# VectorE's queue in a channel mixer: weight decodes placed behind the small steps of the latest w_ch2 scale

## The chip, the cores and the metric

The kernel runs on one core of a Trainium2 chip, in one launch. The metric is the device time of one execution in microseconds. The core's engines each work through a queue of their own in order: TensorE (PE, matmuls; PEld is its weight load), VectorE (DVE), ScalarE (ACT), GpSimd (POOL) and SyncE (SP), which requests the transfers here.

## What is computed

The reference chains a causal attention, a token and channel mixer and a gated mixer (batch 2, 448 tokens, 768 channels, 12 heads). The change touches the channel mixer's second half and the load of the gated mixer's first weight:

```python
u = x + (relu(x.T @ w_tok1) @ w_tok2).T        # x: attention's output, 2 x 448 x 768
y = u + relu(u @ w_ch1) @ w_ch2                # w_ch1 768 x 1536, w_ch2 1536 x 768
h = gelu(y @ w_in)                             # w_in 768 x 1024: halves w_inu and w_inv
u2, v = split(h)                               # v is normalised, mixed over tokens, times u2
out = y + gated @ w_out
```

w_tok1, w_tok2, w_ch1, w_ch2, w_in and w_out arrive as 64-bit floats and are turned into 32-bit ones on the chip; the other inputs are 32-bit.

## The kernel before, in words

A weight is loaded by `decode` (L104): one transfer (L113, on SP) into one of two raw buffers `wraw`, a ScalarE pass (L120) over the high words, and two VectorE instructions, a shift (L123) and a shift with an OR (L124), which joins the low words. L124 is the last reader of the raw buffer, so the transfer after the next waits for it.

For accuracy a product is made of three matmuls (`mm3`, L174 to L181: high by high, high by low, low by high). From the channel mixer's second half on, high and low are fp16 with one scale for a whole slice. `spread` (L156) makes a scale: a small matmul (L158) brings the maxima of all partitions together, then come three small VectorE steps, a maximum (L159), a clamp and product (L160) and a reciprocal (L161). I call them the scale's small steps.

The second half runs over m = 0 to 5, 128 output channels each, and two batches. `channel_down(m, ws, [b])` (L226) is one group of 36 matmuls y_ps (L178 to L180), which reads r (the first half's output, split to fp16) and ws[m], the fp16 halves of slice m of w_ch2. An eviction on VectorE (L233, yt), an addition on GpSimd (L235) and a maximum on VectorE (L146, yam) follow. TensorE's groups come in the order (0,0), (1,0), (0,1), (2,0), (1,1), (3,0), (2,1), (4,0), (3,1), (5,0), (4,1), (5,1), written (m, batch).

A slice of w_ch2 takes two functions. `load_w2(m)` (L546) decodes it in two halves (tiles w2m, four buffers), has ScalarE sum up absolute values (L553), and takes the larger sum (L151, w2am) as the bound. `end_w2(m)` (L557) calls `spread`, which makes scale m, and `split16p` (L168): ScalarE multiplies by the scale (L170) and copies to fp16 (L171), and GpSimd subtracts for the low half (L172).

The loop at L607 interleaves these. In round m it traces: group (m, 0); in round 0 the split of r of batch 1 (`split_r`, twelve splits on ScalarE L165 and VectorE L166); `load_w2(m + 3)`; group (m - 1, 1); `end_w2(m + 2)`; the decode of slice m of w_inv (two in round 4, tile wv, six slices of 512) with its maximum (wvam). After the loop come the scale of w_inv, three slices of w_in's other half (`begin16`, tile wm, maximum wams), the last groups, and `to16(b)`, which spreads the maximum of all y of a batch and splits y. Then the v stage begins (L672).

What sets the order of each engine's queue is a planner: it runs a model of the kernel when the program is built, and of the instructions that are ready in the model it prefers the one traced first. `tc.issue_after(ins)` adds an edge: what the block traces on the engine of `ins` is queued behind `ins`. It makes no engine wait for another, and does nothing to the instructions of other engines.

Of the kernel before, what the change touches and what calls it, by code (L numbers as in the profile page):

```python
# [24 lines left out]
TOP = 32768.0  # L25
# [3 lines left out]
def mixer_kernel(  # L29
# [18 lines left out]
    nc = tc.nc  # L48
# [7 lines left out]
    NCC = C // P  # L56
# [47 lines left out]
    def decode(m, src, twice=False):  # L104


        n = src.shape[-1]
        raw = wpool.tile([P, WC], mybir.dt.int64, tag="wraw", name="wraw", bufs=2)[:, :n]
        if twice:
            nc.sync.dma_start(raw[:64], src)  # L110
            nc.sync.dma_start(raw[64:], src)
        else:
            last_load[0] = nc.sync.dma_start(raw, src).ins  # L113
        words = raw.bitcast(I32).rearrange("p (n w) -> p n w", w=2)
        mi = m.bitcast(I32)

        nc.scalar.activation(  # L120
            m, words.bitcast(F32)[:, :, 1], AF.Prelu, scale=2.0 ** -112, alpha=-(2.0 ** 32)
        )
        nc.vector.tensor_scalar(mi, mi, 3, None, ALU.logical_shift_left)  # L123
        nc.vector.scalar_tensor_tensor(mi, words[:, :, 0], 29, mi, ALU.logical_shift_right, ALU.bitwise_or)  # L124
# [19 lines left out]
    def absmax(dst, src):  # L144

        return nc.vector.tensor_reduce(dst, src, AX.X, ALU.max, apply_absolute_value=True)  # L146

    def top_of(cols, name):

        am = stp16.tile([P, 1], BF16, name=name)  # L150
        last_top[0] = nc.vector.tensor_reduce(am, cols, AX.X, ALU.max).ins  # L151
        return am
# [3 lines left out]
    def spread(pm, am, inv, s, top):  # L156

        nc.tensor.matmul(pm[:, :P], am.to_broadcast([P, P]), ident_b, start=True, stop=True)  # L158
        nc.vector.reduce_max(inv, pm[:, :P], axis=AX.X)  # L159
        nc.vector.tensor_scalar(inv, inv, 1e-20, 1.0 / top, ALU.max, ALU.mult)  # L160
        nc.vector.reciprocal(s, inv)  # L161

    def split16(hi, lo, src, s):

        nc.scalar.activation(hi, src, AF.Copy, scale=s)  # L165
        nc.vector.scalar_tensor_tensor(lo, src, s, hi, ALU.mult, ALU.subtract)  # L166

    def split16p(hi, lo, m, s):  # L168

        nc.scalar.activation(m, m, AF.Copy, scale=s)  # L170
        nc.scalar.copy(hi, m)  # L171
        nc.gpsimd.tensor_sub(lo, m, hi)  # L172
# [40 lines left out]
    def channel_up(m, batches, pool, psum):  # L213

        wh, wl = load_w(w_ch1[m])
        for b in batches:
            us = slice(b * S, (b + 1) * S)
            pr = psum.tile([P, 512], F32, tag="d", name="r_ps")
            mm3(pr[:, :S], [((wh[:, c, :], wl[:, c, :]), (u_hi[c][b], u_lo[c][b])) for c in range(NCC)])
            r = pool.tile([P, S], F32, tag=f"r{m}_{b}", name="r")  # L220
            nc.scalar.activation(r, pr[:, :S], AF.Relu, accum_out=rsum[:, b, m:m + 1])
            r_of[m, b] = r
# [284 lines left out]
    wv32 = wvp.tile([P, NCC, DH], F32, name="wv32")  # L507
# [5 lines left out]
    w2sc = [[sc.tile([P, 1], F32, name=f"w2{n}{m}") for n in ("inv", "s")] for m in range(NCC)]  # L513
    w2sum = sc.tile([P, NCC, 2], F32, name="w2sum")
    yam = sc.tile([P, B, NCC], F32, name="yam")
    wvam = sc.tile([P, NCC], F32, name="wvam")
# [10 lines left out]
    with rs:  # L527
        ps_d = ctx.enter_context(tc.tile_pool(name="ps_d", bufs=8, space=PSUM, reuse_waits="tile"))
        r1pool = rs.enter_context(tc.tile_pool(name="r1pool", bufs=1, reuse_waits="tile"))
        tmp = rs.enter_context(tc.tile_pool(name="tmp", bufs=3, reuse_waits="tile"))  # L530
        def pst(name):
            return ps_d.tile([P, 512], F32, tag="d", name=name)

        def split_r(b):

            am = top_of(rsum[:, b], f"ram{b}")
            spread(pst("rs_ps"), am, *rsc[b], TOP)
            for c in range(NFF):
                if b == 0:
                    t = r1pool.tile([P, 2, S], F16, name=f"r16_{c}")  # L540
                else:
                    t = (rpool if c < NF0 else r1pool).tile([P, 2, S], F16, tag=f"r{c}_0", name=f"r16_{c}")
                split16(t[:, 0], t[:, 1], r_of[c, b], rsc[b][1][:, 0:1])
                r_of[c, b] = t

        def load_w2(m):  # L546

            ms = []
            for i in range(2):
                w = tmp.tile([P, WC], F32, tag="w2m", name="w2m", bufs=4)  # L550
                decode(w, w_ch2[m, :, i * NCC:(i + 1) * NCC, :].rearrange("p a f -> p (a f)"))
                unused = tmp.tile([P, WC], BF16, tag="w2a", name="w2a", bufs=1)
                nc.scalar.activation(unused, w, AF.Abs, accum_out=w2sum[:, m, i:i + 1])  # L553
                ms.append(w)
            w2_begun[m] = ms, top_of(w2sum[:, m], f"w2am{m}")

        def end_w2(m):  # L557

            ms, am = w2_begun.pop(m)
            spread(pst("w2_ps"), am, *w2sc[m], TOP)  # L560
            ws[m] = []
            for i, w in enumerate(ms):
                if m < 2:
                    t = tmp.tile([P, 2, NCC, P], F16, name=f"w2_{m}{i}", bufs=1)
                else:
                    t = wpool.tile([P, 2, NCC, P], F16, tag=("whi", "wlo")[i], name="w2", bufs=3)
                split16p(*(t[:, h].rearrange("p a f -> p (a f)") for h in range(2)), w, w2sc[m][1][:, 0:1])
                ws[m] += [(t[:, 0, c, :], t[:, 1, c, :]) for c in range(NCC)]

        w2_begun, ws, w16, begun = {}, {}, {}, []  # L570
        tail = 4
        for m in [*range(NF0 - tail), *range(NF0, NFF), *range(NF0 - tail, NF0)]:
            channel_up(m, [1] if m < NF0 else [0, 1], r1pool, ps_d)
            if m == NF0 + 1:
                with tc.issue_after(last_load[0]):
                    load_w2(0)
            if m == NFF - 2:
                end_w2(0)
                load_w2(1)
            if m == NF0 - tail:  # L580
                end_w2(1)
                split_r(0)
            if m == NF0 - 1:
                load_w2(2)

        def to16(b):

            spread(pst("ys_ps"), yam16[b], *ysc[b], TOP)
            nc.vector.tensor_mul(vinv[:, 2 * b:2 * b + 1], ysc[b][0], wvsc[0])
            hs = slice(64 * b, 64 * b + 64)  # L590
            nc.vector.tensor_copy(vinv[hs, 1:2], vinv[hs, 2 * b:2 * b + 1])
            for m in range(NCC):
                y16[m][b] = upool.tile([P, 2, S], F16, tag=f"ul{m}_{b}", name=f"y16_{m}_{b}")
                split16(y16[m][b][:, 0], y16[m][b][:, 1], y32[m][b], ysc[b][1][:, 0:1])
                ts = slice((1 - b) * (S - 64), (1 - b) * (S - 64) + 64)
                nc.vector.tensor_copy(y3[:, :, m, 64 * b:64 * b + 64], y16[m][b][:, :, ts])

        def begin16(src, j):

            k = src.shape[1]  # L600
            m = wpool.tile([P, WC], F32, tag="wm", name="wm", bufs=3)[:, :k * P]
            decode(m, src.rearrange("p a f -> p (a f)"))
            am = wams[:, j:j + 1]
            absmax(am, m)
            begun.append((j, k, m, am))

        for m in range(NCC):  # L607
            channel_down(m, ws[m], [0], ps_d, tmp)
            if m == 0:
                with tc.issue_after(mms[0, 0][NFF // 2]):  # L610
                    split_r(1)
            if m + 3 < NCC:
                load_w2(m + 3)
            if 0 < m < NCC - 1:
                channel_down(m - 1, ws[m - 1], [1], ps_d, tmp)
            if m + 2 < NCC:
                end_w2(m + 2)
            for c in ([m], [m], [m], [m], [m, m + 1], [])[m]:
                decode(wv32[:, c, :], w_inv[:, c, :])
                absmax(wvam[:, c:c + 1], wv32[:, c, :])  # L620
            if m == NCC - 2:
                wvam16 = top_of(wvam, "wvam16")
        spread(pst("wv_ps"), wvam16, *wvsc, TOP)
        for c in range(NCC):
            split16(wvh[:, c, :], wvl[:, c, :], wv32[:, c, :], wvsc[1][:, 0:1])
        for m in range(3):
            begin16(w_inu[m], m)
        channel_down(NCC - 2, ws[NCC - 2], [1], ps_d, tmp)
        to16(0)
        channel_down(NCC - 1, ws[NCC - 1], [1], ps_d, tmp)  # L630
        last_y = last_top[0]
# [71 lines left out]
    am = gp.tile([P, 1], BF16, name="sg_am")  # L703
# [125 lines left out]
```

## Time and profile before

| | |
|---|---|
| median of 3 runs | 428.0 us (427.85 to 429.33) |
| the profiled execution | 429.78 us, of which the span is 427.8 us |
| TensorE busy | 396.2 us, 93% of the span |
| VectorE busy | 286.9 us, 67% |
| ScalarE busy | 248.2 us, 58% |
| GpSimd busy | 206.2 us, 48% |
| mean granted TensorE clock | 0.975 of full speed |

The page cuts the span into 40 slices of 10.7 us and gives a busy share for each. Shares over the whole span say little about one stage, so the stage of the second half, 231 to 322 us, is read from the timeline and from tables over stretches. In a timeline a row tells where an instruction began, how long it lasted, its engine, line and tiles, and in brackets how long the engine had been idle ahead of it and what released it.

### The profile page before, as it was taken

Reading aid. Unit: us, or ns where it says so; the run is one execution under the profiler, and the core shown is the slowest. Engines: PE = TensorE matmul, PEld = TensorE weight load, DVE = VectorE, ACT = ScalarE, POOL = GpSimd, SP = SyncE. Lnnn points to the kernel's source line nnn. Section 1 sums busy time; section 2 is a strip of 40 time slices with the busy share of each in tenths; the row PEclk is TensorE's granted clock in tenths of the full one; section 3 lists DMA queues with packets and bytes.
Section 4 is the critical chain, followed back from the end, with each engine's and each line's share of the span. In section 5 each row is a group of like instructions: output and inputs, shape, how many; then the busy total and the mean of one; then the engine's idle time right before and its main releaser. Section 6 shows DMA issues by size and latency. Waiting matters only on the chain.

```text
span 427.8 us, 7292 instructions
## 1 busy us (share of the span) xinstructions
PE 396.2 (93%) x2610; PEld 268.7 (63%) x2610; DVE 286.9 (67%) x689; ACT 248.2 (58%) x481; POOL 206.2 (48%) x211
## 2 busy tenths in 40 slices
PE   5978899797899999999999999996999999999996
PEld 3546687674788999999887545542454445544553
DVE  5969666798945635434357997778696897557832
ACT  3979767587976555654779755434064575661200
POOL 2785848587866573431453145241611566228300
PEclk9989899996999999999999999999799999999999
DMA  7999788999956744665540503455403022100122
GB/s 221 200 299 214 163 155 172 245 262 247 266 120 153 174 145 152 221 223 188 180 149 0 185 13 111 154 169 187 141 0 88 0 100 98 51 1 0 66 106 87
DMA packets 61459, 60.99 MB, mean 143 GB/s; under 512 B 47856, under 2 KB 53104, under 8 KB 61424
## 3 DMA queue, kind: packets, MB, share of 16 engines
q1 hardware_dynamic: 61424, 60.54, 52.5%
q8 instruction: 20, 0.33, 0.3%
q14 instruction: 15, 0.12, 0.1%
HBM read 46.50 MB, written 2.75 MB: 115 GB/s over the span
## 4 chain that ended last, share of the span: by engine, by line
PE 35%; DVE 23%; DMA 15%; issue 9%; POOL 8%; ACT 8%; SPq 1%; POOLq 0%; ACTq 0%; DVEq 0%
DMA wraw<-in 7%; PE r_ps L179 5%; PE r_ps L180 5%; PE r_ps L178 5%; DMA pT<-hl 4%; DMA vr<-in 3%; PE s_ps L330 3%; DVE r L166 3%; DVE pe L335 3%; DVE wm L124 2%; PE o_ps L180 2%; PE o_ps L178 2%; PE o_ps L179 2%; DVE w2m L124 2%; POOL hl L357 2%
## 5 line engine op out<-in xcount | busy, mean ns | idle before, releaser
L330 PE MATMUL s_ps<-k,q 128*128 128x64 f32 (+3 forms) x216 | 59.7, 425 | 8.5 <-DMA q<-in 4.7
L357 POOL TENSOR_TENSOR hl<-pe,hl 128x512 f16<-128x512 f32 x43 | 52.9, 1236 | 27.6 <-ACT hl L356 25.5
L100 POOL TENSOR_TENSOR wlo<-wm,whi 128x768 fp32r<-128x768 f32 x19 | 37.7, 1984 | 42.0 <-ACT whi L133 42.0
L178 PE MATMUL y_ps<-r,w 128*128 128x448 f16 x144 | 51.5, 359 | 4.2 <-ACT w L171 4.2
L178 PE MATMUL r_ps<-uh,whi 128*128 128x448 f32 x144 | 53.6, 372 | 0.0
L179 PE MATMUL r_ps<-ul,whi 128*128 128x448 f32 x144 | 53.3, 370 | 0.0
L180 PE MATMUL r_ps<-uh,wlo 128*128 128x448 f32 x144 | 53.0, 368 | 0.0
L179 PE MATMUL y_ps<-r,w 128*128 128x448 f16 x144 | 51.7, 359 | 1.0 <-DVE r L166 1.0
L180 PE MATMUL y_ps<-r,w 128*128 128x448 f16 x144 | 51.3, 358 | 1.1 <-POOL w L172 1.1
L120 ACT ACTIVATE wm<-wraw 128x768 f32<-128x768 f32 (+2 forms) x35 | 27.9, 797 | 41.0 <-DMA wraw<-in 25.2
L123 DVE TENSOR_SCALAR wm<-wm 128x768 int32<-128x768 int32 (+2 forms) x35 | 20.8, 593 | 44.3 <-ACT wm L120 44.3
L330 PEld LDWEIGHTS s_ps<-k,q 128*128 128x128 f32 x216 | 34.1, 218 | 19.9 <-issue 5.5
L335 DVE CUSTOM_DVE_ANT_0 pe<-s_ps,mask 128x192 f32<-128x192 f32 (+3 forms) x84 | 34.9, 443 | 7.9 <-PE s_ps L330 7.7
L124 DVE SCALAR_TENSOR_TENSOR wm<-wraw,wm 128x768 int32<-128x768 int32 (+2 forms) x35 | 37.4, 1068 | 0.5
L235 POOL TENSOR_TENSOR y<-yt,ul 128x448 f32<-128x448 f32 x12 | 15.1, 1262 | 45.6 <-DVE yt L233 45.6
L344 ACT ACTIVATE pe<-pe,bias 128x448 f32<-128x448 f32 (+3 forms) x74 | 35.3, 526 | 0.3
L381 PE MATMUL x_ps<-vh,pT 128*128 128x65 f16 (+1 forms) x240 | 26.1, 198 | 7.4 <-DMA pT<-hl 6.6
L172 POOL TENSOR_TENSOR w<-w2m,w 128x768 f16<-128x768 f32 x12 | 21.8, 1834 | 22.3 <-ACT w L171 13.2
L356 ACT CAST hl<-pe 128x512 f16<-128x512 f32 x43 | 26.1, 611 | 8.6 <-DMA pT<-hl 7.7
L381 PEld LDWEIGHTS <-pT 128*128 128x128 f16 (+1 forms) x240 | 21.2, 98 | 13.8 <-DMA pT<-hl 8.8
L179 PEld LDWEIGHTS r_ps<-ul,whi 128*128 128x128 f32 x144 | 27.0, 188 | 2.7 <-issue 0.4
L180 PEld LDWEIGHTS r_ps<-uh,wlo 128*128 128x128 f32 x144 | 27.0, 188 | 2.7 <-issue 0.2
(205 smaller groups left out, 1022.7 us busy)
## 6 DMA issues: line engine op xcount, KB each, us to landing
wraw<-in SPq DMA_DIRECT2D x35, 768.0 KB, 4.5
wraw<-in SPq DMA_DIRECT2D x14, 512.0 KB, 3.7
vr<-in SPq DMA_DIRECT2D x12, 320.0 KB, 3.8
k<-in SPq DMA_DIRECT2D x12, 224.0 KB, 3.1
q<-in SPq DMA_DIRECT2D x24, 112.0 KB, 3.2
out<-ob SPq DMA_DIRECT2D x12, 224.0 KB, 1.9
wraw<-in SPq DMA_DIRECT2D x3, 256.0 KB, 3.4
pT<-hl SPq DMA_TRANSPOSE x43, 3.9
```

What stands on the lines that cost most here:

```text
L100: nc.gpsimd.tensor_sub(lo, src, f32(hi))
L120: nc.scalar.activation(m, words.bitcast(F32)[:, :, 1], AF.Prelu, scale=2.0 ** -112, alpha=-(2.0 ** 32))
L124: nc.vector.scalar_tensor_tensor(mi, words[:, :, 0], 29, mi, ALU.logical_shift_right, ALU.bitwise_or)
L178: nc.tensor.matmul(ps, lh, rh, start=i == 0 and not begun, stop=False)
L179: nc.tensor.matmul(ps, lh, rl, start=False, stop=False)
L180: done.append(nc.tensor.matmul(ps, ll, rh, start=False, stop=i == n - 1).ins)
L330: nc.tensor.matmul(ps[:, o:o + m], qp[:, q0:q0 + P], k2[:, ks], start=True, stop=True)
L335: nc.vector.tensor_tensor_reduce(out=pe[:, cs], in0=ps[:, cs], in1=mask0 if i == 0 else mask[:, MASKS[i]], scale=-1.0 / math.sqrt(D), scal ...
L344: nc.scalar.activation(pe[:, cs], pe[:, cs], AF.Exp, bias=bias[:, j:j + 1], scale=-1.0)
L356: nc.scalar.copy(hl[:, 0], pe)
L357: nc.gpsimd.tensor_sub(hl[:, 1], pe, hl[:, 0])
L381: nc.tensor.matmul(o, ph, vh[:, c, h, :D + 1], start=j == 0, stop=False)
```

## The change

`spread` returns its reciprocal, and `end_w2` hands it on. In the loop `load_w2(m + 3)` is traced after group (m - 1, 1) and `end_w2(m + 2)`, no longer before them, and it stands with the w_inv decodes in a block whose VectorE instructions are queued behind the reciprocal of the latest w_ch2 scale. In rounds 4 and 5 that is still scale 5's. The three `begin16` of w_in go behind scale 5's reciprocal too. Nothing is added to or removed from what the engines execute.

```diff
         nc.vector.tensor_scalar(inv, inv, 1e-20, 1.0 / top, ALU.max, ALU.mult)
-        nc.vector.reciprocal(s, inv)
+        return nc.vector.reciprocal(s, inv).ins
...
-            spread(pst("w2_ps"), am, *w2sc[m], TOP)
+            done = spread(pst("w2_ps"), am, *w2sc[m], TOP)
...
+            return done
...
-            if m + 3 < NCC:
-                load_w2(m + 3)
             if 0 < m < NCC - 1:
                 channel_down(m - 1, ws[m - 1], [1], ps_d, tmp)
             if m + 2 < NCC:
-                end_w2(m + 2)
-            for c in ([m], [m], [m], [m], [m, m + 1], [])[m]:
-                decode(wv32[:, c, :], w_inv[:, c, :])
-                absmax(wvam[:, c:c + 1], wv32[:, c, :])
-            if m == NCC - 2:
-                wvam16 = top_of(wvam, "wvam16")
+                spread_last = end_w2(m + 2)
+            with tc.issue_after(spread_last):
+                if m + 3 < NCC:
+                    load_w2(m + 3)
+                for c in ([m], [m], [m], [m], [m, m + 1], [])[m]:
+                    decode(wv32[:, c, :], w_inv[:, c, :])
+                    absmax(wvam[:, c:c + 1], wv32[:, c, :])
+                if m == NCC - 2:
+                    wvam16 = top_of(wvam, "wvam16")
...
-        for m in range(3):
-            begin16(w_inu[m], m)
+        with tc.issue_after(spread_last):
+            for m in range(3):
+                begin16(w_inu[m], m)
```

## Rows read from the trace of the kernel before

**Rows 1.** The page's slices: TensorE's busy tenths and its granted clock.

```profile
PE   5978899797899999999999999996999999999996
PEclk9989899996999999999999999999799999999999
```

**Rows 2.** TensorE's waits, 225 to 345: line, releaser, total us, times, longest.

```profile
PE y_ps L178 <- ACT w L171: 4.2, 1, 4.2
PE y_ps L180 <- POOL w L172: 1.1, 2, 0.9
PE y_ps L179 <- DVE r L166: 1.0, 2, 0.6
```

**Rows 3.** Busy table of tile y_ps, four groups: stretch, us, PE, DVE, PEclk, DMA.

```profile
266.75:273.60 6.85, 6.85 (x37) 0.97 (x2) 1.00 0.70 228
280.50:287.60 7.10, 6.88 (x37) 0.67 (x1) 1.00 0.41 124
...
294.60:308.75 14.15, 9.10 (x37) 1.35 (x2) 0.76 0.51 165
```

**Rows 4.** Timeline of TensorE, 277 to 316.

```profile
280.43 0.22 PE L158 MATMUL w_ps<-ident_b,w2am 128*128 128x128 bf16 x1
...
294.31 0.35 PE L180 MATMUL y_ps<-r,w 128*128 128x448 f16 x1
298.86 0.56 PE L178 MATMUL y_ps<-r,w 128*128 128x448 f16 x1 [4.19 <-ACT w L171]
...
303.98 0.44 PE L180 MATMUL y_ps<-r,w 128*128 128x448 f16 x1
...
315.66 0.22 PE L158 MATMUL ys_ps<-ident_b,yam 128*128 128x128 bf16 x1
```

**Rows 5.** Timeline of VectorE, 280 to 305.

```profile
280.53 0.94 DVE L123 TENSOR_SCALAR wv<-wv 128x512 int32<-128x512 int32 x1 [2.08 <-ACT wv L120]
...
288.10 0.43 DVE L123 TENSOR_SCALAR wv<-wv 128x512 int32<-128x512 int32 x1 [0.87 <-ACT wv L120]
...
292.51 0.68 DVE L233 SCALAR_TENSOR_TENSOR yt<-y_ps,yinv,uh 128x448 f32<-128x448 f32 x1
293.11 0.28 DVE L159 TENSOR_REDUCE w2inv<-w_ps 128x1 f32<-128x128 f32 x1
293.30 1.92 DVE L124 SCALAR_TENSOR_TENSOR wm<-wraw,wm 128x768 int32<-128x768 int32 x1
...
296.13 0.15 DVE L161 RECIPROCAL w2s<-w2inv 128x1 f32<-128x1 f32 x1
...
303.41 0.96 DVE L146 TENSOR_REDUCE wams<-wm 128x1 bf16<-128x768 f32 x1
```

**Rows 6.** Timelines of ScalarE and GpSimd, 293 to 303.

```profile
296.32 1.76 ACT L170 ACTIVATE w2m<-w2m,w2s 128x768 f32<-128x768 f32 x2 [1.84 <-DVE w2s L161]
...
293.27 1.14 POOL L235 TENSOR_TENSOR y<-yt,ul 128x448 f32<-128x448 f32 x1 [7.83 <-DVE yt L233]
298.94 3.62 POOL L172 TENSOR_TENSOR w<-w2m,w 128x768 f16<-128x768 f32 x2 [4.53 <-ACT w L171]
```

**Rows 7.** Timeline of VectorE, 234 to 256.

```profile
234.96 0.78 DVE L123 TENSOR_SCALAR w2m<-w2m 128x768 int32<-128x768 int32 x1 [0.63 <-ACT w2m L120]
...
237.24 0.96 DVE L124 SCALAR_TENSOR_TENSOR w2m<-wraw,w2m 128x768 int32<-128x768 int32 x1
...
240.03 0.15 DVE L161 RECIPROCAL w2s<-w2inv 128x1 f32<-128x1 f32 x1
...
249.43 5.55 DVE L166 SCALAR_TENSOR_TENSOR r<-r,rs,r 128x448 f16<-128x448 f32 x3
```

**Rows 8.** Waits of ScalarE, 225 to 345.

```profile
ACT wv L120 <- DMA wraw<-in: 9.2, 5, 4.0
```

**Rows 9.** TensorE's waits, 340 to 428.

```profile
PE w_ps L158 <- DVE wams L146: 1.0, 1, 1.0
PE gt_ps L158 <- DVE gtam L151: 0.6, 1, 0.6
```

## The prediction

> **What bounds the kernel now.** I read the slices of the page first. TensorE is at nine tenths or more from slice 12 to slice 39, but for slice 28, where it drops to six tenths; its granted clock drops to seven tenths in the slice behind that [rows 1]. So TensorE sets the time of this half, and a change can win only what TensorE loses somewhere. The table of its waits from 225 to 345 us says what it loses there: 4.2 us, once, for ScalarE's fp16 copy of a w_ch2 slice (L171), 1.1 us for GpSimd's rest of one (L172), 1.0 us for the splits of r [rows 2].
>
> Next I cut the stage into its twelve groups of matmuls (a group is one m and one batch, 36 matmuls). An undisturbed group takes 6.85 us; the one from 294.60 to 308.75, which is m = 5 of batch 0, takes 14.15 us at a mean granted clock of 0.76 [rows 3]. **So 14.15 - 6.85 = 7.3 us are lost in this one group.** TensorE's timeline shows how: the last matmul of the group before starts at 294.31, the next at 298.86, after 4.19 us of idle time, and at 298.86 and 303.98 a matmul lasts 0.56 and 0.44 us, against 0.35 at 294.31 [rows 4]. With the 4.2 us and at most 1.1 us of waits [rows 2] 7.3 - 5.3 = 2.0 us or a little more are left: the price of the lower clock behind the idle stretch.
>
> Then I ask why the slice was late. TensorE spread its maximum at 280.43 [rows 4]. VectorE takes that up (L159) only at 293.11, and the reciprocal starts at 296.13 [rows 5]. So 12.7 us pass ahead of the first small step, and 3.0 us within three steps that last 0.15 to 0.28 us. The rows between say why: VectorE's queue holds decodes of w_inv and w_in ahead of L159, and one more between the small steps [rows 5]. These come at the pace of their transfers: ScalarE, which opens each decode, waits 9.2 us in all for raw w_inv data [rows 8], and VectorE stands behind it. After the reciprocal ScalarE scales and copies from 296.32, and GpSimd subtracts twice from 298.94, 3.62 us for both [rows 6]; the first half is whole at 298.94 + 1.81 = 300.75, 4.6 us after the reciprocal began.
>
> **The change part by part.**
>
> *Scale 5 gets ahead of the decodes.* Slices 3, 4 and 5 of w_inv and the three of w_in are queued behind the reciprocal of scale 5. What then stands ahead of its L159 is the eviction of group (2, batch 1), 0.68 us, now at 292.51 [rows 5], which can run as soon as TensorE ends that group near 280.5. The reciprocal then starts at about 280.5 + 0.7 + 0.3 + 0.15 = 281.7, say 282, and the first half is whole at 286.6. TensorE wants it near 294.5. **The two waits and the low clock go, 7.3 us, with 8 us in hand.** ScalarE could eat into that by standing at a raw slice ahead of the scaling; its longest such wait is 4.0 us [rows 8].
>
> *Scale 4 gets ahead of slice 5 and of slice 2 of w_inv.* Group (4, batch 0) lasts 7.10 us with 6.88 busy [rows 3]; these 0.22 us may go. I count nothing.
>
> *Slice 3 of w_ch2 gets behind scale 2.* Now its halves are decoded from 234.96, in some 0.78 + 0.96 us each, and scale 2's reciprocal follows at 240.03 [rows 7]. Afterwards both halves start behind 240, in the window where twelve splits of r for batch 1 are due, and group (0, batch 1) already waits 1.0 us for these [rows 2]. Bounds: below, a gain of 1.0, since ScalarE now stops for the first w_inv slice ahead of the splits; above, both halves get in front of the splits, 2 x 1.74 = 3.5 us. I take 0, the nearer end: the splits are traced earlier than the slice, so that the planner prefers them whenever both are ready, and ScalarE delivers them one right behind another.
>
> *The requests move with the decodes.* Each L113 on SP waits for the L124 that frees one of two raw buffers; their order stays. The edge holds VectorE's part alone: L120 on ScalarE has none. Behind the held decodes wait ScalarE's sum of a slice (L553) and SP, behind which only the loads of b_sg and w_sg are queued. The decodes behind scale 5 could begin at 282 rather than 280.53; at (288.10 - 280.53) / 2 = 3.8 us for a slice [rows 5] the last of w_inv ends near 291 and the last of w_in near 303. TensorE spreads the scale of w_inv behind group (5, batch 0), 301.4 afterwards, and those of w_in in the v stage. No wait follows.
>
> *GpSimd subtracts for scale 5 near 285 to 289*, beside w_inv decodes, not beside the last of w_in. An L124 that starts beside a GpSimd addition takes 1.92 us (293.30 [rows 5], 293.27 [rows 6]), a lone one 0.96 [rows 7]. So a microsecond or two of VectorE's time moves from one place to another, with no TensorE wait behind it.
>
> *Downstream* everything is released by TensorE's own results, and from 340 on it waits only 1.0 and 0.6 us [rows 9]. So the 7.3 us should reach the end.
>
> **Sum.** The profiled run took 429.78 us, 427.80 of it span and 1.98 around it: 427.80 - 7.3 = 420.5 of span, 422.5 with what lies around. The median of the runs shown is 428.00, 1.78 below the profiled run; the same 7.3 taken from it gives **420.7 us**.
>
> **The rivals.**
>
> *The wait moves.* Group (5, batch 0) now ends at 294.5 + 6.9 = 301.4 and (4, batch 1) at 308.25, where TensorE spreads the maximum of batch 0's y (now at 315.66 [rows 4]). That hangs on the eviction of (5, batch 0). If the planner leaves this behind the last w_in slice, whose maximum ends at 303.41 + 0.96 = 304.4 [rows 5], and behind one or two other evictions (0.68 [rows 5], addition 1.14 [rows 6], maximum at most the 0.96 of a w_in slice: 2.8 each), its own 2.8 us end at 310.0 or 312.8, and TensorE waits 1.7 or 4.5 us: 422.4 to 425.2. The other place is the bound above: 3.5 us at the splits of r, 424.2. For it speaks that VectorE's queue runs 12 us behind TensorE's results here (280.5 against 292.51); against it that it is the decodes that hold it up, and that these now come later in the plan, while evictions don't.
>
> *Slower: the w_ch2 slices become one chain.* Slice 3 waits for scale 2, scale 3 for slice 3, and so on to scale 5, whose spread is a matmul in TensorE's queue: if slice 5 is late, TensorE stands there. Eight pieces (two halves each of slices 3, 4 and 5, and two w_inv slices) have to pass between 240.03 [rows 7] and 280.43 [rows 4]. At 4 us each (3.8 by rows 5) plus a pass of ScalarE for the sum, about the 0.88 of one scaling [rows 6], and the maximum, that is 33 of 40 us. If slice 3 only starts behind the splits of r, at 249.4 to 255 [rows 7], the chain ends at 282.6 to 288.2, and TensorE waits 2.2 to 7.8 us, with 2 more for the clock. From 5.3 us of wait on the change loses; at the far end it loses 7.8 + 2 - 7.3 = 2.5 us, and with the two L124 of slice 3 at 1.92 rather than 0.96 a further 1.9: 430.5 to 432.4. For it: the last three splits took 5.55 us [rows 7], so VectorE can be slow there. Against it: not all eight come at the pace of transfers, since a request goes out as soon as a raw buffer is free.
> The Trainium skill (SBUF — State Buffer, section Who interferes with whom) speaks against the change at this place: a VectorE instruction with two SBUF inputs is fully blocked by a GpSimd instruction that reads SBUF, and slice 3's L124 would move from a time in which GpSimd idles to the one in which it subtracts for scale 2. By that rule each L124 would wait out a whole subtraction; the 5.55 us agree with it. The prices above stand without it.
>
> *Given back.* The v stage and the gates behind it become the bound, as VectorE's work there doesn't shrink, and the time stays at 428. Against it: TensorE's short waits from 340 on [rows 9]. The same time comes out if the change doesn't do what it says, which only the planner could bring about: the decodes do stand ahead of scale 5's steps in the queue [rows 5].
>
> **How the numbers follow.** The forecast, 419 to 422: 0.56. The wait moves in part, 422 to 425.8: 0.20. Given back, 425.9 to 430.1: 0.10. Slower, by the chain: 0.14. The measurement can tell about 0.5%, 2.1 us, from no change. So faster is 0.56 + 0.20 = 0.76, same 0.10, slower 0.14. The range begins at 428 - 7.3 - 1.0 - 0.2 = 419.5, less 0.5 for the scatter of the runs, 419.0, and goes to 427.0, which leaves out the slower case and part of the one that gives all back.
>
> **What would show it.** Right: L159 of scale 5 within 2 us of its spread; no wait of TensorE for L171 or L172 over 0.5 us; group (5, batch 0) at 6.9 us with a clock of 1.00; the v stage from about 315. Wrong: a wait of TensorE at a spread of w2am; longer waits for r; evictions of batch 0 behind w_in; new waits once the v stage has begun.

## The result and the profile after

The changed kernel takes 423.45 us (median of 4 runs, 422.21 to 424.69) against 427.93 us before (427.66 to 429.33): a ratio of 0.989, 95% interval 0.985 to 0.993. So it is 4.5 us faster, inside the range on record (419.0 to 427.0), but 2.75 us behind the 420.7 us that were taken as likeliest, and outside the 419 to 422 us that had the highest chance. All ratios here and below leave out single runs that took over 1.5% longer than the fastest run of their kernel, such as 428.01 us in e5 and 433.79 us in e9. Most of the forecast gain came, and part of it was taken away again at another place.

The profiled execution took 422.21 us with a span of 420.1 us. Its span is 7.7 us shorter than that of before, which is more than the medians differ, so I cut both spans at two events: the first y_ps matmul, where the second half of the channel mixer begins, and the first v_ps matmul, where it ends.

| | first y_ps | first v_ps | second half | from there to the end |
|---|---|---|---|---|
| before | 231.2 | 322.5 | 91.3 | 105.3 |
| after | 228.2 | 314.9 | 86.7 | 105.2 |

The part ahead of the first y_ps scatters from execution to execution: it was 228.2 and 229.3 us in two profiles of the changed kernel, 231.2 and 231.7 us in two kernels below that also gain (e1, e2), and 228.4 us in one (e9) whose time is that of before. So the 3.0 us there are within that scatter and are not put down to the change. **The change is worth 91.3 - 86.7 = 4.6 us in the second half**, which agrees with the medians, and this length is what I compare from here on.

The page's slices, TensorE's busy tenths and its granted clock. The 6 in slice 28 and the clock's 7 behind it [rows 1] are gone; a 7 stands in slice 24 now, and a clock of 8 in slice 25:

```profile
PE   5868898796898999999999979999999999999996
PEclk9999999999999999999999998999999999999999
```

TensorE's waits from 225 to 345 us:

```profile
PE w_ps L158 <- DVE w2am L151: 3.0, 1, 3.0
```

The busy table for tile y_ps (stretch, us, PE busy, DVE busy, clock, DMA share, GB/s):

```profile
249.00:260.10 11.10, 8.04 (x36) 0.67 (x1) 0.85 0.35 118
...
280.64:287.50 6.86, 6.86 (x37) 0.68 (x1) 1.00 0.31 93
294.30:301.15 6.85, 6.85 (x37) 0.68 (x1) 1.00 0.63 231
```

All three waits of [rows 2] are gone, and one that was not there before stands in their place. The group that took 14.15 us in [rows 3], (5, batch 0), takes 6.85 us at full clock. But the stretch from 249.00 to 260.10, which holds one group, (2, batch 0), takes 11.10 us at a clock of 0.85: 11.10 - 6.85 = 4.25 us lost. TensorE's timeline shows both parts of that:

```profile
248.64 0.35 PE L180 MATMUL y_ps<-r,w 128*128 128x448 f16 x1
251.99 0.29 PE L158 MATMUL w_ps<-ident_b,w2am 128*128 128x128 bf16 x1 [3.00 <-DVE w2am L151]
252.06 0.58 PE L178 MATMUL y_ps<-r,w 128*128 128x448 f16 x1
252.44 0.58 PE L179 MATMUL y_ps<-r,w 128*128 128x448 f16 x1
```

It stands 3.00 us at the spread of scale 3, which needs the bound of slice 3 (w2am), and then starts matmuls every 0.38 us instead of every 0.19: half speed, the lower of the clock's two levels, for seven matmuls, 7 x 0.19 = 1.3 us. So 7.3 + 1.0 (the splits of r) + 0.2 (group (4, batch 0)) - 4.25 = 4.25 of the 4.6 us.

What was aimed at did happen. VectorE's timeline at scale 5, to be held against [rows 5]:

```profile
280.84 0.68 DVE L233 SCALAR_TENSOR_TENSOR yt<-y_ps,yinv,uh 128x448 f32<-128x448 f32 x1 [2.04 <-PE y_ps L180]
281.44 0.28 DVE L159 TENSOR_REDUCE w2inv<-w_ps 128x1 f32<-128x128 f32 x1
281.75 0.15 DVE L160 TENSOR_SCALAR w2inv<-w2inv 128x1 f32<-128x1 f32 x1
281.94 0.17 DVE L161 RECIPROCAL w2s<-w2inv 128x1 f32<-128x1 f32 x1
```

The spread was at 280.64; one eviction and the three small steps follow without a decode between them, and the reciprocal starts at 281.94 instead of 296.13.

Why is slice 3's bound late? VectorE's timeline of the changed kernel from 246.5 to 252 us:

```profile
246.52 1.87 DVE L166 SCALAR_TENSOR_TENSOR r<-r,rs,r 128x448 f16<-128x448 f32 x3
248.31 0.43 DVE L123 TENSOR_SCALAR wv<-wv 128x512 int32<-128x512 int32 x1
249.75 0.62 DVE L146 TENSOR_REDUCE yam<-y 128x1 f32<-128x448 f32 x1 [1.02 <-POOL y L235]
250.29 1.57 DVE L124 SCALAR_TENSOR_TENSOR wv<-wraw,wv 128x512 int32<-128x512 int32 x1
251.79 0.14 DVE L151 TENSOR_REDUCE w2am<-w2sum 128x1 bf16<-128x2 f32 x1
```

ScalarE's, the second sum of slice 3:

```profile
247.86 0.84 ACT L553 ACTIVATE w2a<-w2m 128x768 bf16<-128x768 f32 x1
248.61 0.19 ACT L553 ACTIVATION_READ_ACCUMULATOR w2a<-w2m 128x1 f32 x1
```

And GpSimd's:

```profile
246.69 3.03 POOL L235 TENSOR_TENSOR y<-yt,ul 128x448 f32<-128x448 f32 x1 [9.54 <-DVE yt L233]
249.69 3.68 POOL L172 TENSOR_TENSOR w<-w2m,w 128x768 f16<-128x768 f32 x2
```

ScalarE has that sum ready at 248.61 + 0.19 = 248.80, just ahead of TensorE, which is free at 249.0. VectorE takes it up only at 251.79. Ahead of it in VectorE's queue stand a maximum that waits for GpSimd's addition, and L124 of the first w_inv slice. So the 3.0 us have the form of the fault that the change removes, small steps behind a decode, two scales earlier. Before, the same L151 ran at 239.26, 5.8 us ahead of TensorE's spread at 245.10; slice 3 was then free of scale 2:

```profile
239.26 0.16 DVE L151 TENSOR_REDUCE w2am<-w2sum 128x1 bf16<-128x2 f32 x1
245.10 0.22 PE L158 MATMUL w_ps<-ident_b,w2am 128*128 128x128 bf16 x1
```

### The profile page after: what moved, and what is told of

It reads as the page before. It is cut to its first block, busy times and chain, and to the rows that moved or that the text cites. A ratio compares the mean times of both kernels' runs of the same rounds, so it can differ in the third digit from the quotient of the medians.

```text
span 420.1 us, 7291 instructions
## 1 busy us (share of the span) xinstructions
PE 389.7 (93%) x2610; PEld 264.0 (63%) x2610; DVE 281.4 (67%) x689; ACT 248.5 (59%) x481; POOL 207.2 (49%) x211
## 3 DMA queue, kind: packets, MB, share of 16 engines
HBM read 46.50 MB, written 2.75 MB: 117 GB/s over the span
## 4 chain that ended last, share of the span: by engine, by line
PE 47%; DVE 13%; DMA 12%; POOL 11%; issue 8%; ACT 6%; SPq 2%; POOLq 0%; ACTq 0%; DVEq 0%
PE r_ps L179 6%; PE r_ps L180 6%; PE r_ps L178 6%; PE y_ps L178 5%; PE y_ps L180 5%; PE y_ps L179 5%; DMA vr<-in 5%; DMA pT<-hl 5%; POOL hl L357 3%; PE o_ps L179 2%; PE o_ps L180 2%; PE o_ps L178 2%; DMA wraw<-in 2%; DVE wm L124 2%; POOL wl L172 2%
## 5 line engine op out<-in xcount | busy, mean ns | idle before, releaser
L357 POOL TENSOR_TENSOR hl<-pe,hl 128x512 f16<-128x512 f32 x43 | 54.0, 1264 | 24.3 <-ACT hl L356 23.8
L330 PE MATMUL s_ps<-k,q 128*128 128x64 f32 (+3 forms) x216 | 54.7, 393 | 11.5 <-DVE mx L335 4.8
L123 DVE TENSOR_SCALAR wm<-wm 128x768 int32<-128x768 int32 (+2 forms) x35 | 21.7, 621 | 42.5 <-ACT wm L120 42.5
L330 PEld LDWEIGHTS s_ps<-k,q 128*128 128x128 f32 x216 | 30.2, 198 | 21.7 <-DVE mx L335 5.7
L235 POOL TENSOR_TENSOR y<-yt,ul 128x448 f32<-128x448 f32 x12 | 15.5, 1290 | 48.4 <-DVE yt L233 45.5
L124 DVE SCALAR_TENSOR_TENSOR wm<-wraw,wm 128x768 int32<-128x768 int32 (+2 forms) x35 | 35.4, 1013 | 0.6
L172 POOL TENSOR_TENSOR w<-w2m,w 128x768 f16<-128x768 f32 x12 | 21.3, 1791 | 15.3 <-ACT w L171 12.6
```

The source lines that it names most:

```text
L330: nc.tensor.matmul(ps[:, o:o + m], qp[:, q0:q0 + P], k2[:, ks], start=True, stop=True)
L357: nc.gpsimd.tensor_sub(hl[:, 1], pe, hl[:, 0])
```

## The experiments

The theory at the start: the gain is group (5, batch 0), 7.3 us, and it comes from the holds behind scale 5; the loss is slice 3's bound, and it comes from the hold behind scale 2. A rival formed on the way, behind e2: any shift of the slices that brings scale 5's steps ahead of the w_in decodes does the same. Another: the new tracing order, not the holds, does it. The table gathers all runs; the lengths are from one profile each, in us, worked out from times rounded to 0.1. "Reciprocal 5" counts from the first y_ps matmul.

| run | what is held | reciprocal 5 | wait at L171 | wait for w2am | second half | ratio to before, 95% |
|---|---|---|---|---|---|---|
| before | nothing | 65.0 | 4.2 | none | 91.3 | 1 |
| after | all rounds, w_in | 53.7 | none | 3.0 | 86.7 | 0.985 to 0.993 |
| e1 | behind scale 5 alone | 54.5 | none | none | 85.2 | 0.988 to 0.995 |
| e2 | rounds 0 to 2 alone | 58.9 | none | 3.0 | 87.0 | 0.979 to 0.992 |
| e3 | all, w_inv slice 0 one scale later | 52.9 | none | 1.2 | 84.6 | 0.978 to 0.988 |
| e4 | all but slice 3 | 51.9 | none | none | 83.7 | 0.978 to 0.992 |
| e5 | as after | 53.9 | none | 3.0 | 86.8 | 0.980 to 0.992 |
| e6 | round 2 alone | 58.7 | none | none | 84.9 | 0.980 to 0.992 |
| e7 | as e4, last w_in slice otherwise | 52.4 | none | none | 83.8 | 0.979 to 0.989 |
| e8 | nothing; own raw buffer for w_inv | 53.4 | none | none | 82.9 | 0.991 to 0.997 |
| e9 | nothing; new tracing order | 64.8 | 4.2 | none | 92.1 | 0.996 to 1.003 |
| e10 | round 1 alone | 65.3 | 4.6 | none | 92.1 | 0.997 to 1.004 |

Twelve groups of 6.85 us would take 82.2 us. The intervals of the kernels that gain mostly overlap, so the second half has to tell them apart. The two profiles of the changed kernel agree in it within 0.3 us, before and e9, which show the same waits, within 0.8; so I take differences of 2 us as real and leave those under 1 us alone. The second half doesn't count what is lost behind the first v_ps: from there to the end it is 105.2 to 105.3 us in most kernels, but 105.8 us in e1, e3, e4 and e6 and 106.3 in e7, where TensorE waits 1.7 to 1.9 us at the spread of batch 1's y. So 0.6 us, and 1.1 in e7, come off what these gain.

**e1, only what follows scale 5 is held.** Slices 3 to 5 of w_ch2 and slices 0 to 2 of w_inv go as before.

```diff
+            if m + 3 < NCC:
+                load_w2(m + 3)
             if 0 < m < NCC - 1:
...
-            with tc.issue_after(spread_last):
-                if m + 3 < NCC:
-                    load_w2(m + 3)
+            with tc.issue_after(spread_last) if m >= NCC - 3 else nullcontext():
```

> Only what follows scale 5 is held behind its reciprocal (slices 3 to 5 of w_inv, three of w_in); rounds 0 to 2 are traced as in the kernel before, so slice 3 of w_ch2 is decoded ahead of scale 2. Theory A (the changed kernel wins 7.3 us at group (5, batch 0) and 1.0 at the splits of r, and loses 3.0 of wait and 1.3 of low clock at the spread of scale 3): 427.9 - 7.3 = 420.6, between 419.8 and 421.5; no wait of TensorE at a spread, waits of 1.0 us for the splits of r as before. Theory B (holding scale 5's followers is worth only the 4.5 us that were measured, the rest is lost further on): 423.5.

Measured: 424.96 us (423.04 to 426.57, 7 runs), second half 85.2 us, with these waits of TensorE from 225 to 345 us:

```profile
PE ys_ps L158 <- DVE yam L151: 2.9, 2, 1.7
PE y_ps L179 <- DVE r L166: 1.1, 2, 0.7
```

The stall at (5, batch 0) is gone without the holds of rounds 0 to 2, and no spread of w2am waits. The waits that come instead, 1.1 us for batch 0's y and 1.75 for batch 1's, are the form that "the wait moves" gave in the prediction. Theory A's time is missed by them: it had no wait at any spread and at most 421.5 us. Counted to the end, this kernel is only 1.5 - 0.6 = 0.9 us ahead of the changed one, too little to tell them apart.

**e2, only rounds 0 to 2 are held.** The w_inv slices 3 to 5 and w_in are free.

```diff
-            with tc.issue_after(spread_last):
+            with tc.issue_after(spread_last) if m < NCC - 3 else nullcontext():
...
-        with tc.issue_after(spread_last):
-            for m in range(3):
-                begin16(w_inu[m], m)
+        for m in range(3):
+            begin16(w_inu[m], m)
```

> The other half alone: rounds 0 to 2 as in the changed kernel, nothing held behind scale 5. Theory A: the spread of scale 3 costs 3.0 + 1.3 us and the splits give 1.0 back, 3.3 us net; if the late reciprocal of scale 5 stays where the transfers put it, at about 296, TensorE comes 3.3 us later to the stall at group (5, batch 0), which shrinks by as much: 428 us; if the decodes shift along, 431.2. Theory B: these rounds cost nothing, 427.9 with no wait at the spread of scale 3.

Measured: 421.72 us (420.94 to 426.1, 4 runs), second half 87.0 us. The wait of 3.0 us for w2am is there, as the theory had it; but the stall at group (5, batch 0), which it had kept, is not. VectorE's timeline at scale 5:

```profile
287.81 0.68 DVE L233 SCALAR_TENSOR_TENSOR yt<-y_ps,yinv,uh 128x448 f32<-128x448 f32 x1
288.40 0.28 DVE L159 TENSOR_REDUCE w2inv<-w_ps 128x1 f32<-128x128 f32 x1
288.77 1.20 DVE L123 TENSOR_SCALAR wv<-wv 128x512 int32<-128x512 int32 x1
289.89 0.14 DVE L160 TENSOR_SCALAR w2inv<-w2inv 128x1 f32<-128x1 f32 x1
290.01 0.69 DVE L124 SCALAR_TENSOR_TENSOR wv<-wraw,wv 128x512 int32<-128x512 int32 x1
290.62 0.15 DVE L161 RECIPROCAL w2s<-w2inv 128x1 f32<-128x1 f32 x1
```

Decodes of w_inv still stand between the steps, but the w_in decodes now stand behind them; in [rows 5] one stood between. That only what is queued behind scale 5 frees this group falls with it, and the two parts of the change don't add up: each removes the same stall.

**e3, slice 0 of w_inv behind scale 3 instead of scale 2.** This takes one decode out of VectorE's queue ahead of slice 3's bound.

```diff
-                for c in ([m], [m], [m], [m], [m, m + 1], [])[m]:
+                for c in ([], [0, 1], [m], [m], [m, m + 1], [])[m]:
```

> The changed kernel, but slice 0 of w_inv is decoded in round 1 (behind scale 3), together with slice 1. Theory A1 (scale 3's maximum is late since VectorE has a decode step of w_inv slice 0 and a maximum of y ahead of it): ScalarE's sum ends near 248.8 and TensorE reaches the spread at 249.0, so the wait falls from 3.0 to under 0.8 us and the clock stays: 427.9 - 7.3 - 1.0 - 0.2 + 0.5 = 419.9. Rival A2 (slice 3 itself is too late because it is held behind scale 2): the wait stays above 2 us, 422.5 to 423.5.

Measured: 421.15 us (420.12 to 423.35, 4 runs), second half 84.6 us. VectorE at scale 3:

```profile
249.09 1.85 DVE L166 SCALAR_TENSOR_TENSOR r<-r,rs,r 128x448 f16<-128x448 f32 x3
251.98 0.62 DVE L146 TENSOR_REDUCE yam<-y 128x1 f32<-128x448 f32 x1 [1.03 <-POOL y L235]
252.51 0.15 DVE L151 TENSOR_REDUCE w2am<-w2sum 128x1 bf16<-128x2 f32 x1
```

TensorE there:

```profile
252.72 0.23 PE L158 MATMUL w_ps<-ident_b,w2am 128*128 128x128 bf16 x1 [1.18 <-DVE w2am L151]
252.78 0.35 PE L178 MATMUL y_ps<-r,w 128*128 128x448 f16 x1
```

L124 no longer stands between, and the wait falls from 3.00 to 1.18 us. That lies between the two forecasts (under 0.8, over 2): the decode is the larger part, not all. What is left is the maximum of y, which still waits 1.03 us for GpSimd. After 1.18 us of idle time the matmuls go on at 0.35 us, at full clock: the second half is 2.1 us shorter, though TensorE now waits 0.92 us at the spread of batch 0's y and 1.75 us at that of batch 1's, the latter behind the second half.

**e4, slice 3 is not held.** It is traced ahead of scale 2's steps again, all else as changed.

```diff
+            if m == 0:
+                load_w2(3)
             if 0 < m < NCC - 1:
...
-                if m + 3 < NCC:
+                if 0 < m < NCC - 3:
                     load_w2(m + 3)
```

> The changed kernel, but slice 3 of w_ch2 is traced ahead of scale 2 in round 0 and not held. Theory A: no wait at the spread of scale 3, the 1.0 us at the splits of r is back or not: 420.0 to 421.0. Theory B (the missing gain lies elsewhere): 423.5.

Measured: 421.47 us (420.14 to 424.45, 4 runs), second half 83.7 us. TensorE's waits from 225 to 345 us:

```profile
PE ys_ps L158 <- DVE yam L151: 1.7, 1, 1.7
PE y_ps L179 <- DVE r L166: 1.1, 2, 0.7
```

VectorE's row of slice 3's bound:

```profile
236.91 0.16 DVE L151 TENSOR_REDUCE w2am<-w2sum 128x1 bf16<-128x2 f32 x1
```

The bound is ready at 237, TensorE spreads it at 242.76 without a wait, and the second half is 3.0 us shorter than with the hold: the 4.25 us at scale 3 are back, and the 1.1 us for the splits of r, which the hold had removed, are there again. **The hold of slice 3 behind scale 2 costs 3 us net in the second half, and 2.4 us counted to the end.** The tracing order alone doesn't: in e9, which has it without holds, no spread of w2am waits. In turn TensorE waits 1.75 us at the spread of batch 1's y, within its v stage: VectorE evicts the last group at 315.48, and at 315.38 in the changed kernel, where TensorE comes to its v stage 2.4 us later. Here VectorE is the engine that is late.

**e5, the changed kernel once more,** beside the runs that follow.

> The changed kernel, once more, on the chip of the runs beside it. From its first profile: second half (first y_ps matmul to first v_ps matmul) 86.7 us against 91.3 before, so 4.6 us less; one wait of 3.0 us at the spread of scale 3 for w2am, followed by about 1.3 us at a lower clock, and none at group (5, batch 0). Theory and rival agree here: the second half should be 86 to 88 us again, and the time 4 to 5 us below the kernel before. If the second half comes out at 89 or more, the first profile was not typical.

Measured: 423.69 us (421.47 to 428.01, 4 runs), second half 86.8 us, the same wait of 3.0 us. Both readings of the changed kernel hold.

**e6, only round 2 is held:** slice 5 of w_ch2 and slice 2 of w_inv behind scale 4.

```diff
-            with tc.issue_after(spread_last):
+            with tc.issue_after(spread_last) if m in (2,) else nullcontext():
...
-        with tc.issue_after(spread_last):
-            for m in range(3):
-                begin16(w_inu[m], m)
+        for m in range(3):
+            begin16(w_inu[m], m)
```

> One hold alone: slice 5 of w_ch2 and slice 2 of w_inv queued behind scale 4's reciprocal (round 2); all else in the old tracing places or free. Theory B, formed from the run with the three holds of rounds 0 to 2: what frees group (5, batch 0) there is that slice 5 comes later, so that scale 5's three steps stand ahead of the w_in decodes in VectorE's queue. Then this hold alone does it: reciprocal of scale 5 at 288 to 291 (296.1 before), wait of TensorE for L171 below 1 us (4.2 before), second half 84 to 87 us (91.3 before), and no wait at a spread of w2am, since slice 3 is free: 421 to 424 us. Theory C: the holds of rounds 0 and 1 did it, by making TensorE 4 us later at the spread of scale 3; then this hold alone leaves the wait at L171 at 3 us or more and the second half at 90 us or more, 426 to 429 us.

Measured: 422.97 us (421.6 to 423.81, 4 runs), second half 84.9 us. VectorE at scale 5:

```profile
286.47 0.28 DVE L159 TENSOR_REDUCE w2inv<-w_ps 128x1 f32<-128x128 f32 x1
...
288.70 0.15 DVE L161 RECIPROCAL w2s<-w2inv 128x1 f32<-128x1 f32 x1
...
291.46 0.56 DVE L123 TENSOR_SCALAR wm<-wm 128x768 int32<-128x768 int32 x1 [1.17 <-ACT wm L120]
```

The first w_in decode stands behind the reciprocal. Of the stall 1.1 us are left, the wait for GpSimd's half of the slice (L172) at 294.57. So this hold alone is enough for what e2 showed: with it the planner puts scale 5's steps ahead of w_in. Theory B's reason, that slice 5 comes later, hardly shows in the trace: counted from the start of the half, the last L124 of slice 5 starts at 43.4 us against 42.9 before, and its bound (L151) at 46.3 against 46.5.

**e7, as e4, with the last w_in slice queued behind batch 0's maximum of y.**

```diff
-        with tc.issue_after(spread_last):
-            for m in range(3):
+        top_y0 = last_top[0]
+        for m in range(3):
+            with tc.issue_after(top_y0 if m == 2 else spread_last):
                 begin16(w_inu[m], m)
```

> The changed kernel with slice 3 of w_ch2 traced ahead and free (as in the run where it was not held), and the third w_in slice queued behind the bf16 copy of batch 0's maximum of y instead of behind scale 5. In that earlier run TensorE waited 1.75 us at the spread of batch 1's y and the second half took 83.7 us. If the w_in decodes in VectorE's queue set that wait, it falls below 0.5 us and the second half takes 82 to 83 us: 1 to 2 us below the run without this edit, near 420 us. If it is the VectorE work of the last groups themselves (evictions, maxima, splits of y), the wait stays at 1.5 to 2 us and the second half at 83.5 to 85 us.

Measured: 422.02 us (421.06 to 423.19, 4 runs), second half 83.8 us; the wait at batch 1's y is 1.85 us, not shorter. VectorE's last row of that slice, and its row of batch 1's maximum:

```profile
308.68 0.95 DVE L146 TENSOR_REDUCE wams<-wm 128x1 bf16<-128x768 f32 x1
318.60 0.16 DVE L151 TENSOR_REDUCE yam<-yam 128x1 bf16<-128x6 f32 x1
```

The slice now comes later, but still ahead of batch 1's maximum. So the edit took no work out of VectorE's way there, and whether the w_in decodes set this wait stays open.

**e8, no hold, but w_inv decodes from a raw buffer of its own.**

```diff
-        raw = wpool.tile([P, WC], mybir.dt.int64, tag="wraw", name="wraw", bufs=2)[:, :n]
+        raw = tmp_of[0].tile([P, 512], mybir.dt.int64, tag="wrawv", name="wrawv", bufs=1)[:, :n] if own else wpool.tile([P, WC], mybir.dt.int64, tag="wraw", name="wraw", bufs=2)[:, :n]
...
-                decode(wv32[:, c, :], w_inv[:, c, :])
+                decode(wv32[:, c, :], w_inv[:, c, :], own=True)
```

(To make room, the attention's mask lies in the attention's own pool.)

> The kernel before with one thing changed: the w_inv slices get a raw buffer of their own instead of taking turns with w_ch2 and w_in in the two shared ones. No hold of any kind. Theory A of the prediction (the queue order ahead of scale 5's steps, paced by the transfers, makes the stall at group (5, batch 0)): if the pace of the transfers matters, w_inv is through before 280 us, fewer decodes stand ahead of scale 5's maximum (L159), the reciprocal comes before 290 us and the wait at L171 falls below 1 us: second half 84 to 86 us, 421 to 423 us. Rival: the planner's order alone decides and puts the w_in decodes ahead of scale 5 all the same; then the reciprocal is at 294 us or later, the wait at L171 stays at 3 us or more and the second half at 89 us or more, 426 to 429 us.

Measured: 426.02 us (424.35 to 428.67, 10 runs), second half 82.9 us, the shortest of all. TensorE's waits from 225 to 345 us:

```profile
PE r_ps L170 <- POOL wlo L90: 1.3, 1, 1.3
PE y_ps L170 <- POOL w L162: 0.6, 1, 0.6
PE r_ps L168 <- ACT whi L123: 0.4, 1, 0.4
```

(Line numbers in this kernel are ten less than in the others.) The stall is gone without any hold: VectorE has w_inv and w_in behind it at 281.7, ahead of scale 5's steps at 287.1. In the queue the decodes still stand ahead of these steps; what counts is that none of them is still to be done when the steps are due, not the hold. But the expected 421 to 423 us did not come. From 180 us to the start of the second half at 234.2 TensorE is busy for 51.58 of 54.00 us, where before it was busy for 51.00 of 51.00 (180 to 231 us). So 2.4 us of the 8.4 gained are paid there. Behind these waits the matmuls go on at half speed:

```profile
229.29 0.47 PE L170 MATMUL r_ps<-uh,wlo 128*128 128x448 f32 x1 [1.27 <-POOL wlo L90]
230.08 0.57 PE L170 MATMUL r_ps<-uh,wlo 128*128 128x448 f32 x1
230.45 0.57 PE L168 MATMUL r_ps<-uh,whi 128*128 128x448 f32 x1
```

Eight of them start every 0.37 us instead of every 0.21, which costs some 1.5 us more. That makes 3.9 us; where the rest of the difference to the 2.6 us of the medians lies was not followed further.

**e9 and e10, two controls:** the new tracing order without holds, and round 1 alone (slice 4 of w_ch2, slice 1 of w_inv behind scale 3).

```diff
-            with tc.issue_after(spread_last):
+            with nullcontext():
...
-        with tc.issue_after(spread_last):
+        with nullcontext():
```

```diff
-            with tc.issue_after(spread_last):
+            with tc.issue_after(spread_last) if m in (1,) else nullcontext():
...
-        with tc.issue_after(spread_last):
-            for m in range(3):
-                begin16(w_inu[m], m)
+        for m in range(3):
+            begin16(w_inu[m], m)
```

> The changed kernel's tracing order without any hold: load_w2 stands behind end_w2 in the loop, but nothing is queued behind a reciprocal. Theory: the gain comes from the holds alone, so this is the kernel before: reciprocal of scale 5 at 295 to 297, a wait of about 4.2 us at L171, second half 90.5 to 92 us, 427 to 430 us. Rival: tracing load_w2 later gives the scale's steps their place by itself; then reciprocal 5 comes before 292 us and the second half takes 84 to 88 us.

> One hold alone: slice 4 of w_ch2 and slice 1 of w_inv queued behind scale 3's reciprocal (round 1). Theory: a hold frees group (5, batch 0) only where it moves the w_in decodes behind scale 5's steps. This one leaves a w_in decode ahead of the reciprocal, so the reciprocal stays at 293 to 296 us, TensorE still waits 2 us or more at L171 and the second half stays at 88.5 to 92 us: 425 to 429 us. Rival: any delay of the slices' chain pulls scale 5's steps forward; then the wait at L171 is below 1 us, the second half 84 to 87 us, 421 to 424 us.

Measured: 428.14 us (427.37 to 433.79, 10 runs) and 428.92 us (428.15 to 432.35, 10 runs), both the time of before. VectorE in e9:

```profile
290.21 0.28 DVE L159 TENSOR_REDUCE w2inv<-w_ps 128x1 f32<-128x128 f32 x1
290.41 1.91 DVE L124 SCALAR_TENSOR_TENSOR wm<-wraw,wm 128x768 int32<-128x768 int32 x1
...
293.22 0.15 DVE L161 RECIPROCAL w2s<-w2inv 128x1 f32<-128x1 f32 x1
```

As in [rows 5], L124 of a w_in slice stands between the small steps. Where it does, the wait at L171 is 4.2 to 4.6 us; where the w_in decodes stand behind the reciprocal (after, e1 to e7), there is none for L171. All runs share this, e8 too, where those decodes are over before scale 5's steps; a hold is one way to get there. Why the planner's order flips with the hold behind scale 4 and not with the one behind scale 3 stays open.

## Why the prediction was right in sign and short in size

*Scale 5 gets ahead of the decodes, 7.3 us: right.* Reciprocal at 281.94 (282 forecast), L159 0.8 us behind the spread, group (5, batch 0) at 6.85 us and full clock. "With 8 us in hand" was right too: counted from the start of the half, e6 starts its reciprocal 58.7 - 53.7 = 5.0 us later, and TensorE comes to group (5, batch 0) 3.1 us earlier (63.0 against 66.1), which together uses up the 8 us; e6 loses 1.1 us and has no drop of the clock. What the prediction did not see is that part of the hold is enough: e6 gets the order with two slices held.

*Scale 4, counted at nothing:* the 0.2 us that it said may go are gone; group (4, batch 0) takes 6.86 us.

*Slice 3 gets behind scale 2, taken as 0 between -1.0 and +3.5: the step that failed.* It costs 3 us net by e4 (2.4 to the end), near the upper end, and by another way than either bound was made of. The bounds were prices at the splits of r, and there the change gained its 1.0 us. The loss is at the spread of scale 3. The prediction followed the slice's halves on VectorE (decoded by 241.25, as early as could be hoped) but not the two steps behind them. On ScalarE the sums stood behind seven splits of r and scale 2's scaling and copies and ended at 248.80. On VectorE the bound stood behind a maximum that waits for GpSimd and behind L124, to 251.79. The reason given for 0, that the splits are preferred, was true, and it is just what makes the slice's bound late.

*The rival "slower: the slices become one chain"* had the right mechanism, a wait at a spread of w2am, at the wrong place. It summed the whole chain to scale 5 and asked whether 33 us fit into 40; the wait is at its first link, scale 3, and the later links have room (spreads 4 and 5 wait for nothing: their bounds start at 262.63 and 274.14, the spreads at 266.96 and 280.64). Nor did slice 3's L124 meet GpSimd: both took 0.96 us, at 238.83 and 240.29, while GpSimd stood idle up to 246.69. It was w_inv's first L124 that ran beside a subtraction, 1.57 us instead of 0.69. At 4.25 us with the clock it stays under the 7.3, so the change gains. The likeliest case left this out, and its list of what would show it wrong named just this wait. "The wait moves" gave 422.4 to 425.2, where the time came out, but not by the waits it was worked out from: those come in e1 (1.1 and 1.75 us) and e3 (0.92 and 1.75 us), not in the changed kernel. So the time lies in the range, but in the stretch that was given a chance of 0.20, and for another reason.

*Requests, subtractions, downstream: right.* The last w_inv maximum ends at 291.1 (291 forecast), the last of w_in at 302.3 (303), and from 340 us on TensorE's waits are the 1.0 and 0.6 us of [rows 9]. The time from the first v_ps to the end is 105.2 us, 105.3 before.

*The profiled span against the medians:* the prediction set the sum against the median, as it should; the two profiled spans alone would have read 7.7 us and seemed to confirm the 7.3.

**A version that may beat both.** The runs point to e4: all holds but slice 3's. Its second half is 3.0 us shorter than that of the changed kernel and 7.6 shorter than before, 1.5 us above twelve undisturbed groups; counted to the end, it gains 2.4 us on the changed kernel. e3 and e7 come near it (1.5 and 1.8 us by the same count). By the times, all three beat the kernel before (intervals from 0.978 to 0.992); against the changed kernel, whose interval overlaps theirs, only these stretches of one profile each speak.

## What to carry to other kernels

Where an engine takes its queue in order, look at every small step on which TensorE hangs, and at what stands just ahead of it: a decode paced by a transfer there costs TensorE its whole wait, and the clock behind it. A hold that clears the way for one such step makes what it holds later, so follow the held work to its own next small step, through every queue it passes (here ScalarE's sum and VectorE's maximum of it), and hold only what has slack there. Compare the length of the stage rather than the whole span where another stage scatters by more than the effect, and look behind the stage's end too: of the 3.0 us that e4 gains in its stage, 0.6 us are lost again just behind it.

## What the runs showed of the hardware

VectorE and GpSimd held each other up more than expected. GpSimd's addition L235 takes 1.13 us alone. Started at 246.69, 0.17 us behind three splits of r on VectorE, it took 3.03 us and ended 0.98 us behind VectorE's last instruction (248.31 + 0.43 = 248.74); in e3, beside the same three splits, 2.70 us. The other way round, three splits take 1.87 us, and 5.55 us [rows 7] where GpSimd's subtractions run beside them (before, from 250.49, 4.00 us for two). So in the first case VectorE then waited for the addition that its own splits had held back, the 1.02 us ahead of the late bound. The Trainium skill (SBUF — State Buffer, section Who interferes with whom) has the rule that a VectorE instruction with two SBUF inputs and a GpSimd instruction that reads SBUF exclude each other. The rows agree; the prediction applied it to L124 alone and not to the addition behind the splits.

Idle times of 1.18 us (e3), 1.11 and 1.75 us (e1) left TensorE's matmuls at full clock; after 3.00 us (after) they went on at half of it. The length of one idle time doesn't settle it, though: in e8 a wait of 0.36 us and, 1.95 us later, one of 1.27 us were followed by eight matmuls at half speed.
